# First block's attention taken by token tile, with keys and values of two heads laid side by side among zeros

## The chip, the cores and the metric

The kernel runs on one core of a Trainium2 chip. The metric is device time in microseconds of one launch, the median of three runs. A core has TensorE (PE in the rows; PEld is its weight load), VectorE (DVE), ScalarE (ACT) and GpSimd (POOL), which run side by side and wait for one another by semaphores, and SyncE (SP), whose queue issues nearly all transfers here.

## The reference

Chunked attention feeds a feed-forward layer with a rational activation, and that feeds a soft mixture of experts. All values are float32, except that the weights `w_in` and `w_out` arrive as float64.

```python
# attention: q, k, v of 4 x 8 heads x 768 x 64; chunks of 32 queries
k_full = concat([mem_k, k[chunk_start - 16 : chunk_end + 8]])   # 8 + up to 56 keys
a = softmax(scale * q_c @ k_full.T);  out = a @ v_full
# 3072 tokens x 512
h = x @ w_in                                                    # 2048 columns
g = (a0 + a1 h + a2 h^2 + a3 h^3) / (1 + |b0||h| + |b1|h^2 + 1e-6)
x = g @ w_out
# soft mixture of 8 experts: softmaxes of x @ phi over tokens and over slots
logits = x @ phi;  slots = softmax(logits, 0).T @ x
y = per expert relu(slots @ w1) @ w2;  out = softmax(logits, 1) @ y
```

## The kernel before

The 3072 tokens are taken in six blocks of 512. Each block has eight steps; a step makes 256 columns of `h` (the tile `h`, two times 128 rows by 512 tokens), runs the rational activation over them, and feeds the result to transposes and to the logits. Attention runs ahead: while block b goes through its steps, the attention of block b + 1 is fed in between in small slices (`at` in the order lists `ord0` and `ord`). A unit of attention is a pair, 256 tokens of 8 heads, thus two token tiles of 128.

The parts that the change and the prediction touch:

- **First attention.** Block 0 has no block ahead of it, so its two pairs (A and B in the list `pre`) run before the first step, with the engines' order written out by hand. `attention` (L151) multiplies 32 queries by 64 keys for one head at a time: 64 rows of contraction, 64 columns (L168). Two heads share the 128 partitions, one in each half, so per pair 64 such products give the scores. Each product in float32 runs as two passes. DVE takes the maximum and subtracts it (L186, L189), ACT takes the exponent (L190), PE turns the result (L208), ACT copies it out (L212), DVE forms sums and their reciprocals (L197 to L199), PE multiplies by the values (L228), DVE normalises (L238), PE turns (L246), and ACT copies into `xt` (L250), the block's x.
- **busy** (L285, `f` in `pre`): products with the identity that only keep TensorE going.
- **First h tile.** After the attention `h_part` (L380) makes the first `h` in one go, 16 passes of 512 columns.
- **Narrowing.** Each step of block 0 needs one float64 piece of `w_in` (letters i for its load, s and t for the first two conversions) and one of `w_out` turned (o, n). A conversion (`f64_narrow`, L303 to L307) is a scaling on ACT, a clamp on DVE, a second ACT pass and a combination on DVE, over a staging buffer `g` of which there are four. A piece is 1 MB in two transfers of 512 KB.
- **wp_sum** (L479, z): phi times the turned piece of `w_out`, two short groups of products with an ACT copy between them.
- **A step**: `a1` is three ACT passes over `h` (L607, L608, L610) and one on DVE, `d1` and `t` are DVE's polynomial (L619, L620, L632, L633) and POOL's product (L585), `a2` two more ACT passes (L624, L625). `h` of the next step is made during the step.

Before the first step the order is by hand; from there a scheduler sets the order by priorities and by pins (`issue_after`: not before a named instruction). Each engine runs its instructions strictly in that order, and the transfers are issued in order on SP.

Of the kernel before, what the change touches and what calls it, by code (L numbers as in the profile page):

```python
# [10 lines left out]
F32 = mybir.dt.float32  # L11
# [8 lines left out]
def float_of_bits(u):  # L20
# [3 lines left out]
KN = {  # L24
    'loads': "q0 q1 v0 i0 v1 c0 i1 o0 q2 v2 o1".split(),
    'pre': "f10 A A f5 B B A A A A B B A A B B A A A A s B B B B A A f2 A B B A s A B B A f2 B s B B B c f4 t t n n".split(),
    'pre2': "i2 o2 i3".split(),
    'ord0': "at a1 z0 s2 h0 d1 at t o3 i4 n1 at a2 y h1 p0 at p1 at at".split(),
    'ord': "at a1 h0 d1 at t a2 y x2 h1 p0 p1 x1 at x3 at at r".split(),
    'ordl': "a1 h0 d1 t a2 x2 h1 p0 p1 x1 x3 r".split(),  # L30
# [16 lines left out]
def tile_chunk_attention__rational__soft_moe(  # L47
# [64 lines left out]
    def bank(shape):  # L112
        return ps_m("m", shape)
# [15 lines left out]

    def load_qk(pair, tq=None, tk=None):  # L130
        if tq is None:
            tq, tk = p_q("q", [P, HP, 2 * P]), p_k("k", [P, HP, 8, WIN])
        SP.dma_start(out=tq, in_=qw[pair])
        for o in (slice(0, HP // 2), slice(HP // 2, HP)):
            SP.dma_start(out=tk[:, o], in_=kw[pair, :, o])
        ahead["q", pair] = tq, tk

    def load_v(pair, tv=None):
        if tv is None:
            t = p_v("v", [P, 2, 4, HP, D])  # L140
            tv = [t[:, n] for n in range(2)]
        for n in range(2):
            SP.dma_start(out=tv[n], in_=vwin[pair, :, n])
        ahead["v", pair] = tv
# [6 lines left out]
    def attention(pair, tile4=None, after=None):  # L151
        tile4 = tile4 or (lambda shape: p_a4("a4", shape))
        after = pair + 1 if after is None else after
        t_first = 2 * pair
        b = (t_first * P) // BLK
        qt, kt = ahead.pop(("q", pair))
        if pair < 2:
            both = ps_h("h", [P, 2, 2, HP, WIN])
            sc = [both[:, par] for par in range(2)]
        else:  # L160
            sc = [bank([P, 2, HP, WIN]) for _ in range(2)]
        for n in range(2):
            for hp in range(HP):
                for c in range(4):
                    for par in range(2):
                        r = slice(D * par, D * par + D)
                        o = P * n + CH * c
                        PE.matmul(  # L168
                            sc[par][CH * c:CH * c + CH, n, hp, :],
                            lhsT=qt[r, hp, o:o + CH],  # L170
                            rhs=kt[r, hp, 4 * n + c, :],
                            start=True, stop=True)
            yield
        if after < NPAIR:
            load_qk(after)
        pr = tile4([P, 2, HP, 2, WIN])
        rsum = []
        for par in range(2):
# [12 lines left out]
            yield  # L191
        pt = tile4([P, 2, HP, P])

# [20 lines left out]

        for part in (turns, sums) if pair < 2 else (sums, turns):
            yield from part()
        vt = ahead.pop(("v", pair))
        if pair < 2:
            both = ps_h("h", [P, 2, 2, HP, D])
            pv = [both[:, par] for par in range(2)]  # L220
        else:
            pv = [bank([P, 2, HP, D]) for _ in range(2)]
        for n in range(2):
# [11 lines left out]
            yield  # L235
        x_tok = tile4([P, 2, HP, 2, D])
        for par in range(2):
# [241 lines left out]
    def wp_sum(i):  # L479
# [11 lines left out]
    xtra = [p_xt("xt", [P, 2048]) for _ in range(2)]  # L491
    early = {"q": xtra[0][:, 0:1024].rearrange("p (h t) -> p h t", h=HP),
             "k": xtra[1].rearrange("p (h c j) -> p h c j", h=HP, c=8),
             }

    def load(what):
        kind, n = what[0], int(what[1])
        if kind == "q":
            if n == 1:
                load_qk(1, early["q"], early["k"])  # L500
            else:
                load_qk(n)
        elif kind == "v":
            load_v(n, [p_S("S", [P, 4, HP, D]) for _ in range(2)] if n == 1 else None)
        elif kind == "c":
            load_constants()
        elif kind == "i":
            load_w_in(n)
        elif kind == "o":
            load_w_turned(n)  # L510

    def convert(what):
        kind, n = what[0], int(what[1])
        if n < NSTEP:
            for _ in {"s": narrow_w_in, "n": narrow_w_turned, "z": wp_sum, "i": load_w_in, "o": load_w_turned}[kind](n) or ():
                pass

    new_xt(0)
    for what in KN["loads"]:
        load(what)  # L520
    gens = {"A": attention(0, after=NPAIR), "B": attention(1, lambda shape: p_T("T", shape), after=NPAIR),
            "s": narrow_w_in(0), "n": narrow_w_turned(0), "t": narrow_w_in(1), "c": constants()}
    for what in KN["pre"]:
# [8 lines left out]
    total = NBLK * NSTEP  # L532
    hs, gt_tile = {}, {}

    hs[0] = ps_h("h", [P, 2, BLK])
    h_part(0, hs[0], 0)
    h_part(0, hs[0], 1)
    for what in KN["pre2"]:
# [51 lines left out]
    def run_step(kk, what):  # L590
# [3 lines left out]
        if what == "at":  # L594
            slice_()
        elif what in ("h0", "h1"):
# [7 lines left out]
        elif what == "a1" and live:  # L604
# [3 lines left out]
            ACT.activation(y, hh, AF.Square, scale=rb1)  # L608
            DVE.scalar_tensor_tensor(s, y, QC, s, ALU.add, ALU.add)  # L609
            ACT.activation(t, hh, AF.Identity, bias=a2, scale=a3)  # L610
            act[kk] = s, t, y
# [262 lines left out]

_INS = ['qw', 'kw', 'vw', 'moe_w_in', 'moe_w_out', 'moe_a', 'moe_b', 'w_turned', 'moe2_phi', 'moe2_w1', 'moe2_w2']
_OUTS = [((3072, 512), 'float32')]


def _lay_out(inputs):
# [19 lines left out]
    qw = q.reshape(B, HP, 2, NP, 256, D).transpose(0, 3, 2, 5, 1, 4).reshape(B * NP, 128, HP, 256)  # L899
    kw = windows(k, mem_k).reshape(B, HP, 2, NP, 8, 64, D).transpose(0, 3, 2, 6, 1, 4, 5)  # L900
    kw = kw.reshape(B * NP, 128, HP, 8, 64)
    vw = windows(v, mem_v).reshape(B, HP, 2, NP, 2, 4, 64, D).transpose(0, 3, 2, 6, 4, 5, 1, 7)
# [5 lines left out]
    phi = np.asarray(inputs["moe2_phi"]).reshape(4, 128, 32).transpose(1, 0, 2).reshape(128, 128)  # L908
    return {**inputs, "moe2_phi": phi, "moe2_w2": w2, "qw": qw, "kw": kw, "vw": vw, "moe_w_in": w_in, "moe_w_out": w_out, "w_turned": w_turned}

# [24 lines left out]
```

## Time and profile before

| | us |
|---|---|
| median of three runs (576.18 to 576.56) | 576.53 |
| profiled execution, its own time | 577.91 |
| span of that execution, first to last instruction | 575.8 |
| PE busy / DVE / ACT / POOL | 540.6 / 456.3 / 427.9 / 122.2 |
| first activation of step 0 (block 0) starts | 38.68 |
| first activation of step 8 (block 1) starts | 133.26 |

The profile gives a page of totals, and the trace behind it answers by time: busy time of each engine in chosen stretches, instructions in order of time, and the chain of waits (the work that ended last, followed back). "Busy" of PE includes modelled ends of its pipelined products. A row of the timeline gives start, duration, engine, line, operation, written tile <- read tiles, shape, count, and in brackets how long the engine sat idle before it and what ended that.

### The profile page before, as it was taken

The page shows a single profiled execution, that of the slowest core. Times are in us where ns is not written, and L with a number is a line of the kernel's source. Part 1 is how long each engine was busy: PE and PEld are TensorE (multiplying, and loading weights), DVE is VectorE, ACT ScalarE, POOL GpSimd, SP SyncE. Part 2 cuts the span into 40 slices and gives each one's busy share as a digit, 9 for nine tenths or more (in the row PEclk, how much of TensorE's full clock was granted, in tenths as well). Part 3 has the DMA queues.
Part 4 walks back from the last instruction along what each step waited for, and adds up shares of the span by engine and source line. Part 5 has one row for each costly group of instructions (what it writes and reads, how often), then busy time and mean ns, then how long its engine had stood idle before and what let it go on. Part 6 is the DMA issues. An engine that isn't in the chain of part 4 may idle for free.

```text
span 575.8 us, 13647 instructions
## 1 busy us (share of the span) xinstructions
PE 540.6 (94%) x5874; PEld 362.1 (63%) x5874; DVE 456.3 (79%) x572; ACT 427.9 (74%) x551; POOL 122.2 (21%) x66
## 2 busy tenths in 40 slices
PE   6799897999999999999999999999999999999991
PEld 6644443557767767677766777776768767643351
DVE  3759988989898999979899799898898978831042
ACT  1489896897978999779787888896888978721132
POOL 0001111213221322313231313132223322300000
PEclk8799898999999999999999999999999999999996
DMA  8997854301125315341432335304349374799948
GB/s 319 361 382 256 279 189 162 137 12 56 56 76 183 129 56 183 115 170 36 161 111 74 114 107 184 110 12 174 110 145 372 106 252 150 268 392 410 409 173 357
DMA packets 28139, 105.80 MB, mean 184 GB/s; under 512 B 3376, under 2 KB 3504, under 8 KB 27056
## 3 DMA queue, kind: packets, MB, share of 16 engines
q1 hardware_dynamic: 26928, 100.74, 48.1%
q0 software_dynamic: 1152, 4.19, 1.8%
q8 instruction: 46, 0.75, 0.5%
q14 instruction: 13, 0.11, 0.0%
HBM read 94.44 MB, written 10.49 MB: 182 GB/s over the span
## 4 chain that ended last, share of the span: by engine, by line
PE 56%; DVE 15%; ACT 14%; DMA 8%; issue 4%; POOL 1%; ACTq 0%; SPq 0%; DVEq 0%; POOLq 0%
PE h L380 28%; DMA g<-in_w_turned_dram 5%; PE m L405 4%; PE m L458 4%; ACT S L607 3%; PE lg L398 3%; ACT S L608 3%; ACT g L406 3%; DVE T L619 3%; PE h L796 2%; PE m L228 2%; DVE T L620 2%; PE lg L833 2%; DMA g<-in_moe_w_in_dram 2%; DVE T L632 2%
## 5 line engine op out<-in xcount | busy, mean ns | idle before, releaser
L380 PE MATMUL h<-xt,win 128*128 128x512 f32 x1012 | 268.5, 414 | 0.7 <-DVE T L620 0.6
L380 PEld LDWEIGHTS h<-xt,win 128*128 128x128 f32 x1012 | 184.1, 188 | 50.9 <-issue 12.3
L585 POOL TENSOR_TENSOR S<-S,S 128x1024 f32<-128x1024 f32 x46 | 112.2, 2440 | 335.1 <-DVE S L609 282.1
L607 ACT ACTIVATE S<-h,ctab 128x1024 f32<-128x1024 f32 x47 | 52.5, 1117 | 38.3 <-PE h L380 37.5
L609 DVE SCALAR_TENSOR_TENSOR S<-S,S 128x1024 f32<-128x1024 f32 x47 | 57.3, 1220 | 24.3 <-ACT S L608 23.7
L619 DVE TENSOR_TENSOR T<-T,h 128x1024 f32<-128x1024 f32 x47 | 57.1, 1215 | 7.6 <-ACT T L610 7.6
L405 PEld LDWEIGHTS m<-ident,T 128*128 128x128 f32 x384 | 43.4, 141 | 29.4 <-issue 14.0
L620 DVE SCALAR_TENSOR_TENSOR T<-T,ctab,h 128x1024 f32<-128x1024 f32 x47 | 59.9, 1274 | 0.7
L632 DVE SCALAR_TENSOR_TENSOR T<-T,ctab,S 128x1024 f32<-128x1024 f32 x46 | 58.6, 1274 | 0.0
L633 DVE SCALAR_TENSOR_TENSOR T<-S,T 128x1024 f32<-128x1024 f32 x46 | 56.1, 1220 | 2.4 <-DVE T L632 0.5
L406 ACT ACTIVATE g<-m 128x512 f32<-128x512 f32 x96 | 53.2, 601 | 6.3 <-PE m L405 6.0
L610 ACT ACTIVATE T<-h,ctab 128x1024 f32<-128x1024 f32 x47 | 57.5, 1223 | 0.0
L625 ACT ACTIVATE S<-S,ctab 128x1024 f32<-128x1024 f32 x47 | 54.5, 1159 | 0.9
L624 ACT ACTIVATE S<-S 128x1024 f32<-128x1024 f32 x47 | 50.5, 1074 | 6.1 <-DVE S L609 6.1
L405 PE MATMUL m<-ident,T 128*128 128x128 f32 x384 | 53.0, 278 | 1.2 <-DVE a L189 1.2
L608 ACT ACTIVATE S<-h,ctab 128x1024 f32<-128x1024 f32 x47 | 52.7, 1121 | 0.9 <-DVE T L632 0.9
L380 PE MATMUL h<-xt,x 128*128 128x512 f32 x64 | 31.4, 621 | 3.6 <-DVE x L307 3.6
L398 PE MATMUL lg<-T,wp 128*32 128x512 f32 x192 | 33.1, 605 | 1.3 <-DVE T L633 0.7
L190 ACT ACTIVATE a<-a 128x512 f32<-128x512 f32 x22 | 13.4, 639 | 16.6 <-DVE a L189 16.6
L458 PE MATMUL m<-g,s 128*32 128x512 f32 x192 | 21.8, 595 | 0.4 <-ACT s L450 0.4
L303 ACT ACTIVATE g<-g 128x1024 uint32<-128x1024 uint32 x16 | 18.7, 1166 | 4.3 <-DMA g<-in_w_turned_dram 4.3
L380 PEld LDWEIGHTS h<-xt,x 128*128 128x128 f32 x64 | 11.2, 191 | 16.3 <-issue 15.1
(218 smaller groups left out, 673.5 us busy)
## 6 DMA issues: line engine op xcount, KB each, us to landing
win<-in_moe_w_dram SPq DMA_DIRECT2D x31, 512.0 KB, 7.3
k<-in_kw_dram SPq DMA_DIRECT2D x22, 512.0 KB, 6.3
v<-in_vw_dram SPq DMA_DIRECT2D x22, 512.0 KB, 5.2
g<-in_moe_w_in_dram SPq DMA_DIRECT2D x16, 512.0 KB, 7.3
g<-in_w_turned_dram SPq DMA_DIRECT2D x16, 512.0 KB, 6.5
x<-in_moe_w_out_dram SPq DMA_DIRECT2D x8, 1024.0 KB, 4.8
out_dram<-win SPq DMA_DIRECT2D x12, 512.0 KB, 5.0
q<-in_qw_dram SPq DMA_DIRECT2D x11, 512.0 KB, 3.8
```

Source lines behind the costliest of these rows:

```text
L380: PE.matmul(tile_[f2] if step == total - 1 else tile_[:, f2, :], lhsT=ww[:, c, f2 * P:f2 * P + P], rhs=xx[:, c, :], start=(n == 0), stop=( ...
L405: st["turn"] = PE.transpose(pb[:, m, f2 * P:f2 * P + P], t_[:, f2, tt * P:tt * P + P], ident)
L406: ACT.activation(gts[b, qd][:, 2 * part:2 * part + 2, 2 * P * o:2 * P * o + 2 * P], pb, AF.Copy)
L585: POOL.tensor_tensor(out, q, w, ALU.mult)
L607: ACT.activation(s, hh, AF.Abs, scale=b0)
L608: ACT.activation(y, hh, AF.Square, scale=rb1)
L609: DVE.scalar_tensor_tensor(s, y, QC, s, ALU.add, ALU.add)
L610: ACT.activation(t, hh, AF.Identity, bias=a2, scale=a3)
L619: DVE.tensor_tensor(t, t, hh, ALU.mult)
L620: behind[kk] = DVE.scalar_tensor_tensor(t, t, a1, hh, ALU.add, ALU.mult).ins
L632: DVE.scalar_tensor_tensor(t, t, a0, w, ALU.add, ALU.mult)
L633: st["t"] = DVE.scalar_tensor_tensor(t, e, 2.0, t, ALU.subtract, ALU.mult, reverse0=True).ins
```

## The change

- **By token tile.** Block 0's attention is done by a new function `attention_first`, once for each of the four token tiles (A, B, C, D in `pre`). Keys and values of a tile are laid into a buffer of twice the width: one head in the upper 64 partitions and the left half, the other in the lower 64 and the right half, zeros elsewhere. One product of 128 rows then serves both heads: 16 products of 128 columns for a tile's scores and 16 for its output, where it took 32 of 64 columns each.
- **Zeros and loads.** `clear` writes the zeros, two half-height memsets for each of eight buffers, one buffer on DVE and seven on POOL. Each key or value tile is loaded by two transfers of 64 partitions (256 KB each).
- **First h tile in halves** (`h_first`, H and J in `pre`): H makes the first half of the tokens once tiles 0 and 1 are done, J the second half, 16 passes of 256 columns each.
- **What is loaded and converted before step 0.** The order of loads is new; `w_in` goes ahead of `w_out`. Before, conversions i0, i1 and the first of `w_out` (n) were whole before step 0, and two more had begun. Now only i0 and i1 are converted before it, and `w_out`'s pieces run one step later, with wp_sum in the next step (Z).
- **Constants** come in one transfer with phi. `stack` is built by fewer instructions. `busy` has products of 256 columns.
- **Pins**: conversions stay behind the first activations of the step, the first slice behind J. From block 2 on each engine's order is unchanged.

```diff
 KN = {
-    'loads': "q0 q1 v0 i0 v1 c0 i1 o0 q2 v2 o1".split(),
...
+    'loads': "Q0 K0 K1 V0 Q1 K2 V1 K3 i0 V2 V3 c0 i1 q2 i2 v2 o0 i3".split(),
...
+    def clear(engine, t):
+        for par in range(2):
+            engine.memset(t[apart[par], 1 - par], 0.0)
...
+            for par in range(2):
+                SP.dma_start(out=t[apart[par], par], in_=src[apart[par]])
...
+    def attention_first(n):
+        o = P * (n % 2)
+        sc = ps_h("h", [P, HP, 2, WIN])
+        for hp in range(HP):
+            for c in range(4):
+                PE.matmul(sc[CH * c:CH * c + CH, hp], lhsT=q_first[n // 2][:, hp, o + CH * c:o + CH * c + CH],
+                          rhs=k_first[n][:, :, hp, c, :], start=True, stop=True)
+        yield
...
+        for hp in range(HP):
+            for c in range(4):
+                PE.matmul(pv[CH * c:CH * c + CH, hp], lhsT=pt[:, hp, CH * c:CH * c + CH],
+                          rhs=v_first[n][:, :, c, hp, :], start=True, stop=True)
+        yield
...
+    def h_first(half):
+        if 0 not in hs:
+            hs[0] = ps_h("h", [P, 2, BLK])
+        o = slice(P // 2 * half, P // 2 * half + P // 2)
...
+            for c in range(NC):
+                pins["PE"] = PE.matmul(to[:, :, o], lhsT=w_f[0][:, c, f2 * P:f2 * P + P], rhs=x[:, c, :, o],
+                                       start=(c == 0), stop=(c == NC - 1)).ins
...
+    clear(DVE, k_first[0])
+    for t in (k_first[1], v_first[0], k_first[2], v_first[1], k_first[3], v_first[2], v_first[3]):
+        clear(POOL, t)
...
-        SP.dma_start(out=ctab[:, 0:4], in_=ca.unsqueeze(0).to_broadcast([P, 4]))
-        SP.dma_start(out=ctab[:, 4:6], in_=cb.unsqueeze(0).to_broadcast([P, 2]))
-        SP.dma_start(out=u_acc[:, 0:NC * NSLOT], in_=phi)
+        SP.dma_start(out=u_all[:, BLK - NC * NSLOT:BLK + 6], in_=cst)
...
-    h_part(0, hs[0], 0)
-    h_part(0, hs[0], 1)
...
+        elif what == "Z":
+            if 0 < kk <= NSTEP:
+                convert("z" + str(kk - 1))
```

TensorE's order at the end of the first attention, before: `a_3`, `T_543` are the normalised outputs of pairs A and B, `h_584` the first h tile.

```order
L208 MATMUL m_445<-ident_106,T_340 128x128 x4
L288 MATMUL lg_463<-ident_106 128x128 x2
L246 MATMUL m_466<-ident_106,a_3_460 128x128 x4
L228 MATMUL h_471<-S_158,T_439 32x64 x32
L228 MATMUL h_471<-S_159,T_439 32x64 x32
L246 MATMUL m_538<-ident_106,a_3_460 128x128 x4
L288 MATMUL lg_547<-ident_106 128x128 x2
L246 MATMUL m_550<-ident_106,T_543 128x128 x4
L246 MATMUL m_556<-ident_106,T_543 128x128 x4
L288 MATMUL lg_569<-ident_106 128x128 x4
L380 MATMUL h_584<-xt_143,win_435 128x512 x8
```

The same place now: `x_126` holds the keys of tile 3, `x_125` and `g_127` are the values of tiles 2 and 3, `a_3` and `a_4` their outputs, `h_423` the first h tile.

```order
L265 MATMUL h_347<-x_126,S_161 32x128 x16
L281 MATMUL m_364<-ident_106,T_336 128x128 x4
L357 MATMUL lg_375<-ident_106 128x256
L281 MATMUL m_382<-ident_106,T_379 128x128 x4
L293 MATMUL h_397<-x_125,S_369 32x128 x16
L301 MATMUL m_417<-ident_106,a_3_414 128x128 x4
L318 MATMUL h_423<-xt_119,win_393 128x4x64 x8
L293 MATMUL h_432<-g_127,S_387 32x128 x16
L301 MATMUL m_451<-ident_106,a_4_449 128x128 x4
L318 MATMUL h_423<-xt_119,win_393 128x4x64 x8
```

The first half of the h tile has moved ahead of tile 3's products with the values and its last transposes; these wait behind it.

ScalarE's order up to the first activation of step 0, before: `g_165` is the second `w_in` piece, `g_168` and `g_179` the first two of `w_out`.

```order
L275 ACTIVATE ctab_108<-ctab_108 128x2
L278 ACTIVATE ctab_108<-ctab_108 128x1
L279 ACTIVATE ctab_108<-ctab_108 128x1
L303 ACTIVATE g_165<-g_165 128x1024
L305 ACTIVATE g_165<-g_165 128x1024
L303 ACTIVATE g_168<-g_168 128x1024
L305 ACTIVATE g_168<-g_168 128x1024
L303 ACTIVATE g_179<-g_179 128x1024
L607 ACTIVATE S_638<-h_584,ctab_108 128x1024
```

And now: `g_169` is the first piece of `w_in`, `g_177` the second, `S_387` tile 3's turned weights, `u_109` holds the constants.

```order
L277 ACTIVATE T_379<-T_379 128x512
L284 ACTIVATE S_387<-m_382 128x512
L372 ACTIVATE g_169<-g_169 128x1024
L374 ACTIVATE g_169<-g_169 128x1024
L305 ACTIVATE xt_119<-m_417 128x16x32
L305 ACTIVATE xt_119<-m_451 128x16x32
L344 ACTIVATE u_109<-u_109 128x2
L347 ACTIVATE u_109<-u_109 128x1
L348 ACTIVATE u_109<-u_109 128x1
L372 ACTIVATE g_177<-g_177 128x1024
L374 ACTIVATE g_177<-g_177 128x1024
L660 ACTIVATE S_514<-h_423,u_109 128x1024
```

The conversion of the first `w_in` piece now stands behind tile 3's copy, and the three passes over `w_out`'s pieces have moved behind the first activation.

## Rows read from the trace of the kernel before

**Rows 1.** Busy time in stretches: block 0 from step 0 on, block 1.

```profile
core 0: us, PE busy (x) PEld busy (x) DVE busy (x) ACT busy (x) POOL busy (x), PEclk, DMA share, GB/s
...
38.68:133.26 94.58, 86.13 (x772) 44.47 (x768) 85.41 (x95) 84.61 (x107) 18.39 (x7) 0.96 0.50 174
133.26:209.00 75.74, 75.33 (x886) 54.28 (x879) 70.60 (x86) 65.70 (x84) 19.29 (x8) 1.00 0.29 99
```

**Rows 2.** Chain of waits, the start: start, us, what.

```profile
1.17 5.70 DMA k<-in_kw_dram
...
6.88 11.52 DMA g<-in_moe_w_in_dram
```

**Rows 3.** Timeline of TensorE: start, us, engine, line, operation, tiles, shapes, count.

```profile
23.44 1.06 PE L288 MATMUL lg<-ident 128*128 128x128 f32 x4
...
27.26 0.66 PE L246 MATMUL m<-ident,a 128*128 128x128 f32 x4
...
29.64 1.06 PE L288 MATMUL lg<-ident 128*128 128x128 f32 x8
...
30.54 7.13 PE L380 MATMUL h<-xt,win 128*128 128x512 f32 x16
...
37.60 0.86 PE L168 MATMUL m<-k,q 64*32 64x64 f32 x64
...
38.96 1.98 PE L380 MATMUL h<-xt,win 128*128 128x512 f32 x4
...
162.78 3.64 PE L458 MATMUL m<-g,s 128*32 128x512 f32 x32
```

**Rows 4.** Timeline of VectorE and ScalarE: first attention, narrowing, first activations.

```profile
9.74 0.69 DVE L186 TENSOR_REDUCE mx<-h 128x8 f32<-128x512 f32 x1
...
11.19 0.63 ACT L190 ACTIVATE a<-a 128x512 f32<-128x512 f32 x1 [9.17 <-DVE a L189]
...
18.90 0.63 DVE L197 TENSOR_REDUCE sm<-a 128x8 f32<-128x512 f32 x1
...
19.77 0.20 DVE L199 RECIPROCAL sm<-sm 128x8 f32<-128x8 f32 x1
...
22.50 1.24 DVE L238 TENSOR_TENSOR a<-h,sm 128x512 f32<-128x512 f32 x2
...
22.83 0.60 ACT L212 ACTIVATE T<-m 128x512 f32<-128x512 f32 x1 [1.08 <-PE m L208]
...
31.14 1.15 ACT L303 ACTIVATE g<-g 128x1024 uint32<-128x1024 uint32 x1
...
31.80 0.70 DVE L304 TENSOR_SCALAR g<-g 128x1024 f32<-128x1024 f32 x1
...
32.54 1.13 ACT L305 ACTIVATE g<-g 128x1024 f32<-128x1024 f32 x1 [0.24 <-DVE g L304]
...
33.70 1.23 DVE L307 SCALAR_TENSOR_TENSOR win<-g 128x1024 uint32<-128x1024 uint32 x1 [1.20 <-ACT g L305]
...
38.68 1.10 ACT L607 ACTIVATE S<-h,ctab 128x1024 f32<-128x1024 f32 x1
...
133.26 1.12 ACT L607 ACTIVATE S<-h,ctab 128x1024 f32<-128x1024 f32 x1
```

**Rows 5.** Busy time in stretches of 2 us of the first attention, columns as in rows 1.

```profile
18.00:20.00 2.00, 0.61 (x56) 0.45 (x41) 1.86 (x7) 1.77 (x3) 0.00 (x0) 0.82 0.56 184
...
22.00:24.00 2.00, 2.00 (x11) 2.00 (x10) 1.93 (x6) 0.92 (x2) 0.00 (x0) 0.50 1.01 383
...
26.00:28.00 2.00, 1.95 (x103) 1.69 (x97) 0.64 (x2) 0.05 (x1) 0.00 (x0) 0.97 1.04 422
```

**Rows 6.** Groups by line and shape on GpSimd: count, busy us, mean ns.

```profile
L760 POOL MEMSET wp<- 128x512 f32 x1 | 0.5, 528 | 6.4 <-PE lg L398 6.4
```

**Rows 7.** Timeline in block 0: a wait for a transfer and the one it caused.

```profile
90.88 1.18 ACT L303 ACTIVATE g<-g 128x1024 uint32<-128x1024 uint32 x1 [3.42 <-DMA g<-in_w_turned_dram]
...
97.66 1.06 PE L380 MATMUL h<-xt,x 128*128 128x512 f32 x1 [3.56 <-DVE x L307]
```

More of the change, by code (lines that the diff above doesn't have):

```diff
@@ L149, in new_xt, with attention @@
         xt[b] = [p_xt("xt", [P, NC, BLK], F32R if b else F32) for _ in range(2 if b else 1)]
-    def attention(pair, tile4=None, after=None):
-        tile4 = tile4 or (lambda shape: p_a4("a4", shape))
-        after = pair + 1 if after is None else after
+    def attention(pair):
+        after = pair + 1
         t_first = 2 * pair
@@ L156, in attention @@
         qt, kt = ahead.pop(("q", pair))
[L157 to L161, printed above, removed]
+        sc = [bank([P, 2, HP, WIN]) for _ in range(2)]
         for n in range(2):
@@ L175, in attention @@
             load_qk(after)
[L176 removed]
+        pr = p_a4("a4", [P, 2, HP, 2, WIN])
         rsum = []
@@ L191, in attention @@
             yield
-        pt = tile4([P, 2, HP, P])
+        pt = p_a4("a4", [P, 2, HP, P])
         def sums():
@@ L213, in turns @@
             yield
-        for part in (turns, sums) if pair < 2 else (sums, turns):
-            yield from part()
+        yield from sums()
+        yield from turns()
         vt = ahead.pop(("v", pair))
[L218 to L222, printed above, removed]
+        pv = [bank([P, 2, HP, D]) for _ in range(2)]
         for n in range(2):
@@ L489, in wp_sum @@
         ACT.activation(wp[:, 2 * i:2 * i + 2, :], pb, AF.Copy)
[L491 to L494, printed above, removed]
     def load(what):
         kind, n = what[0], int(what[1])
[L498 to L510, printed above, removed]
+        if kind in "QKV":
+            load_first(kind, n)
+        else:
+            {"q": load_qk, "v": load_v, "c": lambda n: load_constants(), "i": load_w_in, "o": load_w_turned}[kind](n)
     def convert(what):
@@ L514, in convert @@
         if n < NSTEP:
-            for _ in {"s": narrow_w_in, "n": narrow_w_turned, "z": wp_sum, "i": load_w_in, "o": load_w_turned}[kind](n) or ():
-                pass
-    new_xt(0)
+            with tc.issue_after(pins[0]) if 0 in pins else nullcontext(), tc.issue_after(pins[1]) if 0 in pins else nullcontext():
+                for _ in {"s": narrow_w_in, "n": narrow_w_turned, "z": wp_sum, "i": load_w_in, "o": load_w_turned}[kind](n) or ():
+                    pass
     for what in KN["loads"]:
         load(what)
-    gens = {"A": attention(0, after=NPAIR), "B": attention(1, lambda shape: p_T("T", shape), after=NPAIR),
-            "s": narrow_w_in(0), "n": narrow_w_turned(0), "t": narrow_w_in(1), "c": constants()}
+    gens = {"ABCD"[n]: attention_first(n) for n in range(4)}
+    gens.update({"H": h_first(0), "J": h_first(1), "s": narrow_w_in(0), "t": narrow_w_in(1), "c": constants()})
     for what in KN["pre"]:
@@ L594, in run_step @@
         if what == "at":
-            slice_()
+            with tc.issue_after(pins["PE"]) if kk == 0 else nullcontext():
+                slice_()
         elif what in ("h0", "h1"):
@@ L608, in run_step @@
             ACT.activation(y, hh, AF.Square, scale=rb1)
-            DVE.scalar_tensor_tensor(s, y, QC, s, ALU.add, ALU.add)
-            ACT.activation(t, hh, AF.Identity, bias=a2, scale=a3)
+            pins[0] = DVE.scalar_tensor_tensor(s, y, QC, s, ALU.add, ALU.add).ins
+            pins[1] = ACT.activation(t, hh, AF.Identity, bias=a2, scale=a3).ins
             act[kk] = s, t, y
@@ L908, in _lay_out @@
     phi = np.asarray(inputs["moe2_phi"]).reshape(4, 128, 32).transpose(1, 0, 2).reshape(128, 128)
-    return {**inputs, "moe2_phi": phi, "moe2_w2": w2, "qw": qw, "kw": kw, "vw": vw, "moe_w_in": w_in, "moe_w_out": w_out, "w_turned": w_turned}
+    cst = np.concatenate([phi] + [np.tile(np.asarray(inputs[n]), (128, 1)) for n in ("moe_a", "moe_b")], axis=1)
+    return {**inputs, "cst": cst, "moe2_w2": w2, "qw": qw, "kw": kw, "vw": vw, "moe_w_in": w_in, "moe_w_out": w_out, "w_turned": w_turned}
 def kernel(**inputs):
```

118 lines of the change are left out of this document (81 added, 37 removed).

## The prediction

> **What bounds the kernel now.** I read the stretches first. In block 1 PE is busy 75.33 of 75.74 us [rows 1], and from block 2 on no engine's order changes: what counts is when PE comes to its dense work, and how much it stands still on the way. In block 0, from its first activation at 38.68 to that of block 1 at 133.26 [rows 4], no engine is full: PE 86.13, DVE 85.41 and ACT 84.61 of 94.58 us [rows 1]. The three hand work to one another, so about 8 to 10 us stand idle on each. One piece of that has a name: ACT waits 3.42 us for a piece of `w_out`, and behind it PE 3.56 us for weights that DVE combines late [rows 7]. Ahead of block 0 the chain of waits shows transfers alone: one issued at 1.17 and landed at 6.87, the next issued at 6.88 and landed at 18.40 [rows 2]. By order of the loads 1024 KB had landed by then and 5120 KB by the second, so 512 KB take 11.53 / 8 = 1.44 us. On the engines the first h tile runs from 30.54 to 37.67, and that of step 1 starts at 38.96 [rows 3].
>
> **The products themselves.** A pair's half of scores, 64 passes of 64 columns, takes 0.86 us [rows 3]. The new form is 32 passes of 128 columns by 128 rows and 32 weight columns. The nearest row is L458, with the same 128 rows and 32 weight columns: 32 passes of 512 columns in 3.64 us [rows 3], 4500 columns per us, which gives 4096 / 4500 = 0.91 us. So half as many instructions stream as many columns in as much time; between 0.43 (time goes by instructions) and 1.72 (the columns of two heads no longer overlap) I take 0.9. [...]
>
> **The first attention, step by step.** Durations [rows 3, 4]: products 0.9; maximum and subtraction 1.45 (9.74 to 11.19); exponent 0.63; four transposes 0.65; copy 0.60; sums 1.07 (18.90 to 19.97); normalising 0.62; narrowing 1.15 + 1.13 on ACT and 0.70 + 1.23 on DVE. Loads land at 1.44 us per 512 KB from 6.9 on: keys 1 at 8.3, keys 2 with queries at 12.7, keys 3 at 15.5, the first `w_in` piece at 18.4, values 3 at 21.3. A memset of 512 columns takes 0.53 on POOL [rows 6]; 14 of 1024 columns, at twice that, end at 16, before the values they belong to, so the zeros cost nothing. (On a slower POOL, at 1.5 each, they would end at 22, still before tile 3's values are used.)
> Tile 0: scores 6.9 to 7.8, subtracted by 9.35, exponent 10.0, turned 10.65. ACT works in order, so its copy waits for tile 1's exponent (11.45) and ends at 12.05; values 12.95, normalised 13.6. PE then does tile 2's scores (13.85), turns tile 1 (14.5) and tile 0's output (15.15); tile 1's values 16.05, normalised 16.7, turned 17.35. Tile 3's scores end at 18.25, subtracted 19.7, exponent 20.35, turned 21.0, copied 21.6. Only then does ACT come to the first `w_in` piece, landed 3 us before: 22.75, second pass 23.9, DVE's combination 25.1. H follows. A pass of 512 columns takes 7.13 / 16 = 0.45 us [rows 3], so 256 take at least 0.22; with the weight loads closer together I take 0.25, H 4.0 us, to 29.1. Behind H: tile 3's values 30.0, normalised 30.65, turned 31.3, copied 31.9, J to 35.9. In that time ACT does the constants (0.9) and both passes of the second `w_in` piece, to 35.1, DVE's combination to 36.3. The first activation starts at 35.9, not 38.68. PE does the first scores of the next pair (0.86) and starts step 1's h at 36.8, not 38.96: **2.2 us earlier**. Bounds: H and J at 0.22 a pass give 3.1; the other end is the clock, below.
>
> **What block 0 has to take over.** Three ACT passes (2 x 1.15 + 1.13 = 3.4 us) and on DVE three clamps and one combination (2.1 + 1.2), less one combination that falls into block 1, thus 2.1 us, move behind the first activation. They cost between nothing (10.0 us on ACT and 9.2 on DVE are idle there [rows 1]) and 3.4; as both engines are about 90% full, I take half, 1.7. The last wp_sum moves into block 1 and is paid there by a PE that is full: no gain. Against this, `w_in` pieces are now asked for ahead of `w_out`, and the conversion of `w_out` has a step more. SP's queue holds the piece of step 3 and then that of step 4 before the second of `w_out`. The wait of 3.4 to 3.6 us [rows 7] should go; between 0 and 3.6 I take 3.0, since the next to come late, DVE with its 9.2 us of slack, is near. Block 0 gives **1.3 us**. The one transfer of constants in place of three, the shorter `stack` and the pins lie before 6.9 us or beside waits for transfers: nothing.
>
> **The sum.** 2.2 + 1.3 = 3.5 us. The profiled execution took 577.91 us (span 575.8 and 2.1 around it), so it would take 574.4; it stands 1.4 above the median of the runs, 576.53, which becomes 573.0.
>
> **Rivals.**
> *H at half clock: slower.* H starts after PE has had little to do, and tile 3's last products stand behind it in PE's order. [...] At half clock H's passes take 0.43, not 0.25: 2.9 us more for H, as much for J. If 19 of the 32 passes run so, the 3.5 us are gone; with all, the median is 573.0 + 5.8 = 578.8. Against it: there is product work in every 2 us up to H. [...]
> *Twice the product time: slower.* If the 128-row products take 1.72, seven of the eight lie on the chain above, 7 x 0.8 = 5.7 us: median 578.7. L458 speaks against it.
> *Given back: no change.* If ACT is what bounds block 0, the whole 3.4 us lands, and of the wait for `w_out` only 1.2 comes free, as it turns into one for ACT: 2.2 - 3.4 + 1.2 = 0, 576.5. For it: of ACT's 10.0 us of idle time in block 0 [rows 1] a third is that one wait [rows 7], so the rest of the time it is fuller than DVE or PE. Against it: ACT's moved passes spread over eight steps.
> *More: block 0 flows.* If early weights take away half to all of PE's 8.45 us of idle time [rows 1], it gives 4 to 8 us in place of 1.3: 566.5 to 570.3. DVE's and ACT's fill speaks against it.
>
> **How the numbers follow.** Forecast 0.53 (569.8 to 575.3), more 0.16, given back 0.13 (within 0.2%, about what a measurement of this kernel can tell from no change: 575.4 to 577.7), half clock 0.14, doubled products 0.04. Faster 0.69, same 0.13, slower 0.18. The range 567.0 to 578.8 reaches through the clock rival's full price and most of "more" and leaves out about 2 in 10.
>
> **What would show it.** Step 0's first activation near 36, step 1's h near 37. A granted clock near 1.0 in the stretch of H (25 to 29) and rows of 0.25 for its passes against the clock rival; 32 passes of L265 in 0.9 us against the doubled products. Block 0 from first activation to first activation about 93 us, no wait of ACT for `w_out` above 1 us. The forecast is wrong if DVE or ACT idles in block 0 less than now and yet the block takes 95 us or more, or if the first activation lies past 38.

## The result and the profile after

The changed kernel takes 584.72 us (median; 584.23 to 589.53), the kernel before 576.54 on the same chip: ratio 1.0147, 95% interval 1.0114 to 1.0179. It is 1.5% slower, above the whole range of the prediction. The profiled execution took 585.19 us, 7.3 more than the one before.

The starts of the first activations divide the loss; "first" is that of step 0.

| us | before | after | difference |
|---|---|---|---|
| first | 38.68 | 42.52 | +3.84 |
| block 0 (step 0 to step 8) | 94.58 | 94.59 | 0.0 |
| steps 8 and 9 | 19.78 | 21.06 | +1.3 |
| steps 10 to 15 | 58.29 | 60.21 | +1.9 |
| blocks 2 to 5 and the end, to the last instruction | | | +0.5 |

Stretches of the kernel after; columns are stretch, length, busy time (and count) of PE, PEld, DVE, ACT, POOL, then granted clock, DMA share and GB/s. First three stretches of the prologue, one of H, then block 0, steps 8 and 9, steps 10 to 15:

```profile
6.00:8.00 2.00, 0.96 (x32) 0.84 (x32) 0.00 (x0) 0.00 (x0) 1.91 (x3) 1.00 1.04 229
12.00:14.00 2.00, 0.90 (x32) 0.84 (x32) 1.90 (x5) 1.00 (x2) 1.91 (x3) 1.00 1.03 231
16.00:18.00 2.00, 1.70 (x35) 1.30 (x28) 1.38 (x2) 0.91 (x2) 0.00 (x0) 1.00 1.01 231
...
30.00:32.00 2.00, 1.89 (x7) 1.34 (x6) 0.77 (x1) 0.60 (x1) 0.00 (x0) 0.50 1.01 395
...
42.52:137.11 94.59, 87.10 (x844) 44.86 (x843) 89.67 (x99) 87.27 (x108) 16.66 (x7) 1.00 0.53 182
137.11:158.17 21.06, 18.97 (x212) 13.64 (x211) 18.71 (x22) 17.49 (x23) 5.66 (x2) 0.92 0.22 77
158.17:218.38 60.21, 59.39 (x697) 41.90 (x703) 53.45 (x67) 51.09 (x66) 14.44 (x6) 1.00 0.28 97
```

The first and the last two of them in the kernel before:

```profile
6.00:8.00 2.00, 0.46 (x32) 0.33 (x32) 0.00 (x0) 0.00 (x0) 0.00 (x0) 1.00 1.03 414
...
133.26:153.04 19.78, 19.78 (x222) 14.09 (x215) 18.92 (x23) 16.86 (x22) 4.84 (x2) 1.00 0.25 82
153.04:211.33 58.29, 57.88 (x697) 41.87 (x702) 53.90 (x66) 50.98 (x66) 14.45 (x6) 1.00 0.29 100
```

Three things are to be seen. In the prologue the DMA engines are as busy as before (share above 1.0) and move 229 to 231 GB/s, not 414 (or the 422 of [rows 5]). In steps 8 and 9 PE stands still for 2.1 us and its clock is 0.92. In steps 10 to 15 PE does the same work with the same count of products (697), but is busy 1.5 us longer.

The chain of waits at the start (start, us, what) answers to [rows 2]; the transfer of tile 2's values lands at 15.16 + 11.66 = 26.82:

```profile
6.10 9.04 DMA xt<-in_kw_dram
15.16 11.66 DMA x<-in_vw_dram
```

PE's timeline behind that (as [rows 3]): values of tile 2, H, values of tile 3, J, the next pair's scores, step 1's h.

```profile
26.96 1.94 PE L293 MATMUL h<-x,S 128*32 128x128 f32 x32 [2.27 <-DMA x<-in_vw_dram]
29.70 1.11 PE L301 MATMUL m<-ident,a 128*128 128x128 f32 x4 [0.81 <-DVE a L297]
30.92 4.67 PE L318 MATMUL h<-xt,win 128*128 128x256 f32 x16
35.52 1.08 PE L293 MATMUL h<-g,S 128*32 128x128 f32 x32
...
38.76 3.72 PE L318 MATMUL h<-xt,win 128*128 128x256 f32 x16 [0.69 <-ACT xt L305]
42.41 0.86 PE L158 MATMUL m<-k,q 64*32 64x64 f32 x64
43.30 3.24 PE L449 MATMUL h<-xt,win 128*128 128x512 f32 x7
```

H stood behind tile 2's values, for which PE waited 2.27 us. It then ran its first 2.0 us (30.92 to 32.90) at a granted clock of 0.50 and took 4.67 us, where J takes 3.72 at 1.00.

### The profile page after: what moved, and what is told of

The parts are those of the page before. It is cut to its first block, busy times and chain, and to the rows that moved or that the text cites. A ratio compares the mean times of both kernels' runs of the same rounds, so it can differ in the third digit from the quotient of the medians.

```text
span 583.3 us, 13135 instructions
## 1 busy us (share of the span) xinstructions
PE 541.5 (93%) x5604; PEld 360.3 (62%) x5604; DVE 457.7 (78%) x561; ACT 428.1 (73%) x551; POOL 134.5 (23%) x80
## 4 chain that ended last, share of the span: by engine, by line
PE 54%; DVE 18%; ACT 15%; issue 5%; DMA 4%; POOL 2%; SPq 1%; ACTq 0%; DVEq 0%; POOLq 0%
PE h L449 25%; PE m L527 4%; PE m L474 4%; ACT S L660 3%; ACT S L661 3%; PE lg L467 3%; ACT g L475 3%; DVE S L662 3%; DVE T L673 3%; DVE T L672 3%; PE h L852 2%; PE m L214 2%; PE lg L889 2%; DVE T L685 2%; DMA x<-in_vw_dram 2%
## 5 line engine op out<-in xcount | busy, mean ns | idle before, releaser
L449 PE MATMUL h<-xt,win 128*128 128x512 f32 x996 | 259.2, 409 | 1.7 <-issue 0.8
L449 PEld LDWEIGHTS h<-xt,win 128*128 128x128 f32 x996 | 181.0, 188 | 49.3 <-issue 11.1
L660 ACT ACTIVATE S<-h,u 128x1024 f32<-128x1024 f32 x47 | 52.5, 1118 | 40.9 <-PE h L449 38.0
L673 DVE SCALAR_TENSOR_TENSOR T<-T,u,h 128x1024 f32<-128x1024 f32 x47 | 59.8, 1272 | 0.7
L685 DVE SCALAR_TENSOR_TENSOR T<-T,u,S 128x1024 f32<-128x1024 f32 x46 | 58.6, 1274 | 0.0
L663 ACT ACTIVATE T<-h,u 128x1024 f32<-128x1024 f32 x47 | 57.5, 1224 | 0.0
L678 ACT ACTIVATE S<-S,u 128x1024 f32<-128x1024 f32 x47 | 54.3, 1156 | 1.0
L661 ACT ACTIVATE S<-h,u 128x1024 f32<-128x1024 f32 x47 | 52.7, 1122 | 0.6 <-DVE T L685 0.6
L467 PE MATMUL lg<-T,wp 128*32 128x512 f32 x192 | 38.3, 604 | 1.8 <-DVE T L686 1.3
L374 ACT ACTIVATE g<-g 128x1024 f32<-128x1024 f32 x16 | 18.6, 1160 | 2.3 <-DVE g L373 2.3
```

What stands on the lines that cost most here:

```text
L449: PE.matmul(tile_[f2] if step == total - 1 else tile_[:, f2, :], lhsT=ww[:, c, f2 * P:f2 * P + P], rhs=xx[:, c, :], start=(n == 0), stop=( ...
L660: ACT.activation(s, hh, AF.Abs, scale=b0)
L663: pins[1] = ACT.activation(t, hh, AF.Identity, bias=a2, scale=a3).ins
L673: behind[kk] = DVE.scalar_tensor_tensor(t, t, a1, hh, ALU.add, ALU.mult).ins
```

## The experiments

All were timed in alternation with the kernel before, whose median beside them was 576.5 to 577.9 us; so runs are compared by the ratio to it. Stretches are of one profiled execution each.

| | median | ratio (95%) | first | block 0 | steps 8-9 | steps 10-15 |
|---|---|---|---|---|---|---|
| before | 576.54 | | 38.68 | 94.58 | 19.78 | 58.29 |
| after | 584.72 | 1.0147 (1.0114 to 1.0179) | 42.52 | 94.59 | 21.06 | 60.21 |
| e1 two queues | 585.28 | 1.0139 (1.0107 to 1.0172) | 44.40 | 92.27 | 20.70 | 60.21 |
| e2 before, key halves | 580.44 | 1.0051 (1.0032 to 1.0069) | 41.92 | 93.50 | 19.78 | 58.35 |
| e3 values ahead of H | 581.83 | 1.0075 (1.0048 to 1.0101) | 39.64 | 92.03 | 20.73 | 60.23 |
| e4 old conversions | 589.96 | 1.0221 (1.0162 to 1.0279) | 41.72 | 98.84 | 19.13 | 60.23 |
| e5 even and odd partitions | 583.09 | 1.0083 (1.0061 to 1.0105) | 40.83 | 94.20 | 21.37 | 60.67 |
| e6 quartets whole | 589.22 | 1.0199 (1.0157 to 1.0241) | 43.88 | 95.15 | 22.62 | 58.22 |
| e7 before, quartets whole | 579.44 | 1.0032 (1.0016 to 1.0048) | 39.39 | 94.51 | 19.71 | 58.56 |
| e8 e3 + e5 + e6 | 581.00 | 1.0052 (1.0032 to 1.0072) | 36.31 | 93.97 | 22.18 | 58.19 |
| e9 wp_sum's copy first | 586.25 | 1.0142 (1.0121 to 1.0163) | 44.16 | 94.16 | 20.01 | 60.49 |
| e10 e8 + e9, blocks 0, 1 | 578.52 | 1.0015 (1.0001 to 1.0029) | 37.93 | 93.57 | 16.53 | 62.75 |
| e11 fill ahead of H | 592.34 | 1.0223 (1.0186 to 1.0260) | 46.45 | 98.65 | 16.14 | 65.30 |
| e12 e3 + e5 | 578.52 | 1.0013 (0.9994 to 1.0032) | 36.23 | 92.04 | 20.72 | 60.24 |
| e13 e12 + block 1's quartets | 575.58 | 0.9965 (0.9946 to 0.9983) | 36.06 | 92.04 | 20.75 | 58.09 |
| e14 e13 + e9 | 575.09 | 0.9952 (0.9933 to 0.9971) | 37.50 | 92.06 | 19.99 | 58.32 |

After, e6 and e9 have the same order on every engine up to step 0, and their first activations lie at 42.52, 43.88 and 44.16: what is under 1.7 us in that column is not told from chance in one execution.

### The transfers: e2, e1, e5

e2 cuts the first keys by partitions in the kernel before (`D` is 64, `P` 128).

```diff
-        for o in (slice(0, HP // 2), slice(HP // 2, HP)):
-            SP.dma_start(out=tk[:, o], in_=kw[pair, :, o])
+        for o in [(slice(0, D),), (slice(D, P),)] if pair < 2 else [(slice(0, P), slice(0, HP // 2)), (slice(0, P), slice(HP // 2, HP))]:
+            SP.dma_start(out=tk[o], in_=kw[(pair,) + o])
```

> The kernel before, with one edit: the four 512 KB transfers of keys (pairs 0 and 1) are cut by partitions, 64 x 2048, and not by heads, 128 x 1024: the same bytes, number, size and queue. Ports theory: 2 MB at 230 in place of 414 GB/s take 4.1 us more, the first w_in piece lands at 22.4 and not at 18.4, the first activation comes at 42.7 and not at 38.7, and the kernel takes 580 to 581 us. Size theory: the pieces are as large as before, so nothing changes, 576.5.

Windows of e2, of the keys and after them:

```profile
6.00:8.00 2.00, 0.27 (x2) 0.14 (x2) 0.00 (x0) 0.00 (x0) 0.00 (x0) 1.00 1.04 223
...
16.00:18.00 2.00, 1.00 (x62) 0.76 (x57) 0.00 (x0) 0.00 (x0) 0.00 (x0) 0.50 1.02 404
```

Same bytes, number, size and queue: 223 GB/s while the halves move, 404 afterwards, first activation 3.2 us and the kernel 0.51% later. By the landings in the traces a half of 512 KB took 2.3 to 2.5 us here; in the kernel before 512 KB to 128 partitions took 1.3. The size theory falls.

e1 asks for the upper halves from ACT's queue.

```diff
-                SP.dma_start(out=t[apart[par], par], in_=src[apart[par]])
+                (ACT if par else SP).dma_start(out=t[apart[par], par], in_=src[apart[par]])
...
-    start.enter_context(tc.manual_schedule(engines={e.engine for e in (PE, ACT, DVE, POOL)}))
+    start.enter_context(tc.manual_schedule(engines={e.engine for e in (PE, ACT, DVE, POOL, SP)}))
```

> The changed kernel; of each first tile of keys and values the upper 64 partitions are asked for from ACT's queue and the lower 64 from SP's, so that both are under way at once; SP's order is otherwise kept. Ports theory (a transfer to 64 partitions moves at about 230 GB/s, one to 128 at about 414, both read in the traces): the windows from 4 to 20 us go back to about 400 GB/s, the values of tile 2 land near 20 and not at 26.8, step 0's first activation comes at 37 to 38 and not at 42.5, and the kernel takes 579 to 581 us, since block 1 keeps its loss. Size theory (the 256 KB pieces are slow because they are small and at most eight are outstanding): nothing changes, 230 GB/s, 42.5, 584.7. Order theory (H waits for its weights and tile 3's values stand behind it): the loads get faster, but the first activation stays above 41 and the time above 583.

```profile
6.00:8.00 2.00, 0.00 (x1) 0.03 (x1) 0.00 (x0) 0.00 (x0) 1.91 (x3) 0.98 1.01 244
...
12.00:14.00 2.00, 0.85 (x11) 0.30 (x2) 1.38 (x2) 0.00 (x0) 1.91 (x3) 1.00 1.06 287
```

In these windows the rate is 244 and 287 GB/s (the second also holds queries for 128 partitions). The twelfth half lands at 19.74, in the kernel after at 19.51, and the time is that of the kernel after: two halves that are under way together still don't add up to a whole. My form of the ports theory was wrong in that. At most 287 GB/s were measured, against 414 to 422 for transfers to 128 partitions in the kernel before. The eight of the size theory are in the trace: in the kernel after at most eight of SP's transfers lie between issue and landing at a time.

e5 puts one head on the even and the other on the odd partitions. The tiles are cleared whole ahead of the transfers, q is laid out on the host to match, and DVE writes the subtracted scores interleaved.

```diff
-                SP.dma_start(out=t[apart[par], par], in_=src[apart[par]])
+                SP.dma_start(out=t[par:P:2, par], in_=src[apart[par]])
...
```

> The changed kernel with the two heads of a pair on even and odd partitions and not on the lower and upper 64: each transfer still brings 256 KB to 64 partitions, as many and as large, but spread over all 128. The tiles are cleared whole ahead of their transfers, keys of tiles 0 and 1 by DVE, and DVE writes the subtracted scores interleaved. The order of PE's work is the same as in the changed kernel from block 0 on. Ports theory: windows from 6 to 18 us at about 400 GB/s, the values of tile 2 in by 18 to 20, step 0's first activation at 37 to 39 (42.5 before this edit), and the kernel at 579.5 to 581, since the loss of blocks 0 and 1 stays. Rival (a transfer to 64 partitions is slow whichever they are): 230 to 250 GB/s as before, first activation 42 to 44, 584 to 587.

```profile
6.00:8.00 2.00, 0.94 (x32) 0.84 (x32) 0.00 (x0) 0.00 (x0) 2.00 (x2) 1.00 0.72 229
...
12.00:14.00 2.00, 2.00 (x8) 1.43 (x7) 1.90 (x6) 0.92 (x2) 0.00 (x0) 0.50 0.94 350
14.00:16.00 2.00, 2.00 (x50) 1.58 (x52) 1.11 (x5) 0.21 (x1) 0.00 (x0) 0.70 0.95 356
16.00:18.00 2.00, 1.72 (x36) 1.30 (x25) 1.78 (x3) 0.68 (x2) 0.00 (x0) 1.00 0.98 342
...
20.00:22.00 2.00, 2.00 (x41) 1.63 (x42) 1.18 (x4) 0.60 (x1) 0.00 (x0) 1.00 1.04 407
```

Still 64 partitions and 256 KB a transfer, now 342 to 356 GB/s at shares of 0.94 to 0.98, and 407 from 20 to 22, when values of tiles 2 and 3 land, a transfer every 0.64 us (every 1.1 in the kernel after). From 6 to 8 the engines are busy for 0.72 alone: the transfers are issued behind the zeros, which now fill whole tiles. So it is which partitions, not how many: 64 neighbouring ones were filled at 223 to 231 GB/s, every second one at 342 to 407. Why that is so, no run here shows. The kernel won less than expected (583.09, not 581; first activation at 40.83, not 37 to 39). PE waited 1.62 us for H's weights, and H took 5.38 us behind that wait, most of it at a low clock (0.71 granted from 28 to 30, 0.50 from 30 to 32, 0.93 from 32 to 34):

```profile
28.53 5.38 PE L318 MATMUL h<-xt,win 128*128 128x256 f32 x16 [1.62 <-DVE win L377]
```

### The order of H: e3, e11

```diff
-D C C f1 D D D s C C s C C H H D D D D J J c t t
+D C C f1 D D D s C C s C C D D H H D D J J c t t
```

> The changed kernel with tile 3's values and their normalising ahead of the first half of h in the hand-written order. Order theory: tile 3's products, 1.1 us, run while H waits for its weights, the chain behind H loses products, normalising and turning, and the first activation comes 2 us earlier, at 40.5; 582.7 us. Ports theory: those values land late as well (about 29 us), so at most 1 us is saved: 41.5 to 42.5, 583.7 to 584.7.

PE's timeline in e3:

```profile
30.02 1.08 PE L293 MATMUL h<-g,S 128*32 128x128 f32 x32
31.03 3.72 PE L318 MATMUL h<-xt,win 128*128 128x256 f32 x16
34.59 0.60 PE L301 MATMUL m<-ident,a 128*128 128x128 f32 x4
35.88 3.72 PE L318 MATMUL h<-xt,win 128*128 128x256 f32 x16 [0.69 <-ACT xt L305]
```

The values of tile 3 landed in time; tile 3's products fill the wait, H follows at once and takes 3.72 us, as J did at a granted clock of 1.00, and J comes 2.9 us earlier. Block 0 is 2.5 us shorter as well, in e3 and in e12 to e14 alike, where the scheduler's order of block 0 differs too. Other runs separate this from the earlier end of tile 3: e1 leaves tile 3's values behind H, has another order in block 0 and takes 92.27; e5 has the order of the kernel after there, starts 1.7 us earlier and takes 94.20; e8 and e10 have tile 3's values ahead of H and yet other orders, and take 94.0 and 93.6. The length goes with the scheduler's order.

e11 fills the wait with eight idle products (16 passes) instead (`C C f8 H H`).

> The changed kernel with eight idle passes of 256 columns on PE ahead of the first half of h, in the time in which PE waits for its weights. Clock theory (H runs at half clock because PE had little to do, and this is the loss): H takes 3.7 us and not 4.67, as J does; the first activation comes 1 to 3 us earlier, at 39.5 to 41.5. Ports theory: H gets to the full clock, but the loads still set its start and that of J; the first activation moves by 1 us at most, 41.5 to 42.5, and the kernel stays at 583.5 to 585.

```profile
30.97 5.10 PE L357 MATMUL lg<-ident 128*128 128x256 f32 x16
35.90 3.62 PE L318 MATMUL h<-xt,win 128*128 128x256 f32 x16
```

H is fast, as the clock theory says, but the idle products themselves took 5.10 us and pushed H back by 5; first activation and kernel lie above what either theory expected. The low clock of H costs 1 us; buying it off with idle work cost more.

### Block 1: e4, e9, e6, e7

In steps 8 and 9 of the kernel after, PE (first) waits for ACT (second), which waits for POOL: the last `wp_sum` (L552, L554, L557).

```profile
141.79 0.63 PE L552 MATMUL m<-win,u 128*32 128x256 f32 x8
142.25 1.02 PE L467 MATMUL lg<-T,wp 128*32 128x512 f32 x2
145.35 0.92 PE L557 MATMUL m<-stack,s 128*128 128x32 f32 x4 [2.09 <-ACT s L554]
146.20 2.05 PE L158 MATMUL m<-k,q 64*32 64x64 f32 x128
```

```profile
143.91 1.11 ACT L660 ACTIVATE S<-h,u 128x1024 f32<-128x1024 f32 x1 [1.60 <-POOL S L637]
144.93 0.38 ACT L554 ACTIVATE s<-m 128x256 f32<-128x256 f32 x1
```

e4 takes the conversions of block 0 back to the old order (lists `loads`, `pre`, `pre2`, `ord0`, `ord`).

> The changed kernel with the order of block 0's conversions of before: the first w_out piece is narrowed ahead of block 0 again, the others a step earlier, wp_sum in the step of its own piece, and the last wp_sum again inside block 0. Spill theory (block 1's 3.2 us come from the last narrowing and wp_sum that fall into it): block 1 goes back from 81.3 to about 78 us, the first activation stays near 42.5 to 44, and the kernel takes 581 to 583 us. Rival (block 1's stall is the scheduler's order of steps 8 and 9 or the attention's, not that piece): block 1 stays near 81 and the kernel at 584 to 587.

Steps 8 and 9 take 19.13, so the spill is one cause; but steps 10 to 15 stay at 60.23, and block 0 takes 98.84, 4.2 more than after. The kernel, 589.96, lies above both ranges. Taking the deferral back, which I had priced as a cost of 1.7 us, was no gain; where e4 loses in block 0 was not followed.

e9 only orders ACT: the copy ahead of step 9's activation.

```diff
-        ACT.activation(part, pb, AF.Copy)
+        st["ws"] = ACT.activation(part, pb, AF.Copy).ins
...
-            ACT.activation(s, hh, AF.Abs, scale=b0)
+            with tc.issue_after(st["ws"]) if kk == NSTEP + 1 else nullcontext():
+                ACT.activation(s, hh, AF.Abs, scale=b0)
```

> The changed kernel with one rule more: on ACT, the first activation of step 9 (L660) is issued behind the copy of the last wp_sum (L554). In the changed kernel it stands ahead of it and waits 1.60 us for POOL, the copy behind it, and PE, whose second half of wp_sum needs the copy, stands still for 2.09 us and then works at a lower clock (0.88 in that step); steps 8 and 9 take 21.06 us, 19.78 in the kernel before. Spill theory: that wait of PE falls under 1 us, steps 8 and 9 take 19.5 to 20.3, and the kernel 583 to 583.8. Rival (whatever holds PE there is replaced by the next: POOL, DVE's narrowing): steps 8 and 9 stay at 21, 584.7.

PE in e9 at the same place:

```profile
143.46 1.02 PE L467 MATMUL lg<-T,wp 128*32 128x512 f32 x2
144.41 0.63 PE L557 MATMUL m<-stack,s 128*128 128x32 f32 x4
144.97 1.48 PE L158 MATMUL m<-k,q 64*32 64x64 f32 x128
```

No wait, a granted clock of 1.00 in the two steps (the 128 passes of scores take 1.48 and not 2.05 us), and 20.01 for them: the spill theory holds for 1.0 us. The kernel's time doesn't show it (ratio 1.0142, 1.0147 after); the stretch does. In the profiled execution the first activation came 1.6 us later than after.

The rest is in the slot logits, four products of 32 weight columns that can run beside one another. Each shows as two rows. First after, then before:

```profile
195.85 1.04 PE L467 MATMUL lg<-T,wp 128*32 128x512 f32 x2
196.83 0.66 PE L198 MATMUL m<-ident,a 128*128 128x128 f32 x4
197.42 1.06 PE L467 MATMUL lg<-T,wp 128*32 128x512 f32 x6
```

```profile
190.84 1.06 PE L398 MATMUL lg<-T,wp 128*32 128x512 f32 x8
```

One product alone takes 1.04 us, three take 1.06, and all four 1.06. The scheduler's new order breaks the quartets more often. Groups by line, after (L467) and before (L398); count, busy us, mean ns, idle before:

```profile
L467 PE MATMUL lg<-T,wp 128*32 128x512 f32 x192 | 38.3, 604 | 1.8 <-DVE T L686 1.3 <-DVE T L766 0.6
```

```profile
L398 PE MATMUL lg<-T,wp 128*32 128x512 f32 x192 | 33.1, 605 | 1.3 <-DVE T L633 0.7 <-DVE T L710 0.6
```

5.2 us more for the same 192 passes: five pieces more, all ahead of block 2, two of them in steps 10 to 15 (six where there were four). e6 and e7 write the quartets in another order, in the kernel after and before.

```diff
-                for j in range(4):
+                for j in (2, 3, 0, 1):
```

> The changed kernel with one token changed: the four products of a quartet of slot logits (L467) are written in the order 2, 3, 0, 1, so that the one that is written first is one whose operand comes last, and the scheduler has no reason to start the quartet early and break it. In the traces a broken quartet takes 1.05 us for each piece, and a whole one 1.06; the changed kernel has 5 pieces more than the kernel before, all ahead of block 2. Quartets theory (block 1's 3.2 us are 3 such pieces on a full PE, and 2 more fill block 0): L467's sum over the kernel goes from 38.3 to about 33 us, block 1 goes from 81.3 to about 78, the first activation stays at 42 to 43, and the kernel takes 580 to 581.5. Spill theory (the last wp_sum in block 1 makes the loss): block 1 stays at 80 to 81, the kernel at 583 to 585.

> The kernel before with the same token changed (its L398). Its quartets are broken 2 and 2 once in block 0, and once a block in blocks 1 to 5 with 1 and 3. Quartets theory: two pieces fewer ahead of block 3, 2 us of PE time, one of them in full blocks: 574.5 to 575.5. Spill theory: no change, 576.5.

```profile
L467 PE MATMUL lg<-T,wp 128*32 128x512 f32 x192 | 29.7, 604 | 6.5 <-DVE T L686 5.9 <-DVE T L766 0.6
```

In e6 the quartets' sum fell by 8.6 us (5 were expected) and steps 10 to 15 by 2.0; but ahead of the quartets PE now waits 5.9 us for DVE (2.4 of it in blocks 2 to 5, 1.7 in the last steps; 1.3 in the whole kernel after), and in steps 8 and 9 the wait for `wp_sum` grew from 2.1 to 2.9 us, since pieces of a quartet had filled part of it. Both kernels got slower. Only in steps 10 to 15 of e6 was the token a gain.

### Together: e8, e10, e12 to e14

> The changed kernel with heads on even and odd partitions, tile 3's values ahead of H, and the quartets of logits in the order 2, 3, 0, 1. If both theories hold the gains add: first activation at 36 to 37.5, block 0 at 92 to 94, block 1 at 78: 574 to 576, under the kernel before. If only the ports theory holds: 578 to 580. If only the quartets theory holds: 578.5 to 580.

> The changed kernel with heads on even and odd partitions, tile 3's values ahead of H, the rule on the last wp_sum, and the quartets of logits in the order 2, 3, 0, 1 in blocks 0 and 1 alone (in later blocks that order made PE wait for DVE). First activation 36.3 to 37.5, steps 8 and 9 at 19.5 to 20.5 (22.2 with the quartets and without the rule), steps 10 to 15 at 58.2, the later blocks as in the kernel before: 574 to 576, under the kernel before by 0.2 to 0.6%. If the rule on wp_sum doesn't hold: 577 to 579.

e8's 581.00 lies above all three ranges. Its first activation at 36.31 is 6.2 us earlier than after, where e5 and e3 alone give 1.7 and 2.9: together the prologue's two edits win more than apart. Its 22.18 shows that the token hurts elsewhere. In e10 the stall left steps 8 and 9 (16.53) and came back behind them (62.75): 79.28 together, 2 under after, 1.2 above before, and the kernel's 578.52 misses 574 to 576.

> The changed kernel with only the two edits of the prologue: heads on even and odd partitions, and tile 3's values ahead of H. If the prologue's and the later losses are apart from one another: first activation 36.3 to 37.9, block 0 at 92 (as with tile 3's values ahead alone), steps 8 to 15 still at 81, so 575 to 577, the time of the kernel before, or 0.2% under it. If what the prologue gains is taken up by block 0 (94 to 95): 577.5 to 579.

> The same, with the quartets of logits of block 1 alone in the order 2, 3, 0, 1; all of PE's order up to step 8 and nearly all from block 2 on are as in the kernel without it. Quartets theory (broken quartets cost 1.9 us in steps 10 to 15): steps 10 to 15 take 58.2 in place of 60.2, nothing else moves: 1.5 to 2.5 us less than the kernel without it. Rival (with the quartets whole, PE waits for DVE as it did when all blocks had the order): less than 0.7 us less.

> The same with, besides, the rule on the last wp_sum (copy ahead of step 9's first activation on ACT). Steps 8 and 9 a further 1 us shorter (19.7 to 20.2) if the stall doesn't come back in step 10: 573 to 574.5. If the next wait takes its place, as it did when the rule and the quartets of blocks 0 and 1 were together: the same time as without the rule.

Steps 10 to 15 in e12 and in e13:

```profile
148.99:209.23 60.24, 60.24 (x696) 41.96 (x702) 54.05 (x68) 51.08 (x66) 14.44 (x6) 1.00 0.29 97
```

```profile
148.85:206.94 58.09, 56.97 (x725) 42.01 (x724) 54.75 (x68) 51.30 (x66) 14.46 (x6) 1.00 0.29 101
```

e12 undoes the prologue's loss: first activation 36.23, block 0 92.04, and the kernel is level with the one before. Its median lies in the range of the other case, though block 0 did not take the gain up: step 16 begins 2.1 us earlier than before, and part of that goes at the end, where the closing stores took 6.1 us each from issue to landing in place of 5.0. That was not followed. e13 changes one token for block 1: PE was full for 60.24 of 60.24 us and is busy 56.97 now, 2.2 us less in the stretch and 2.9 in the median. That settles the quartets for steps 10 to 15; the median moved by more than the range of 1.5 to 2.5. e14 with the rule on ACT is 0.48% faster than the kernel before (0.29 to 0.67%); over e13 it gains 0.8 us in steps 8 and 9 and nothing that the medians can tell apart, the second of its two cases.

## Why the prediction was wrong

**The step that failed** is the pace of the loads. I read 1.44 us per 512 KB from transfers to 128 partitions [rows 2] and used it for transfers to 64, which took 1.1 us per 256 KB. Tile 2's values should have landed near 19.8 and landed at 26.82; H was to start at 25.1 and started at 30.92; the first activation was to come at 35.9 and came at 42.52. The diff showed the 64 partitions, and the trace of before had no such transfer among the big ones: the price had to be bounded from both sides, and I took one end for it without saying so.

The pace is not the whole of it. e5 spreads the loads and keeps the forecast's order of H; H started at 28.53 and the first activation came at 40.83. Of the 5.8 us by which H was late, that gives back 2.4. Of the 3.4 left, some 1.2 are e5's own: its zeros fill whole tiles, and tile 1's keys, issued behind them, landed at 9.50, not 8.3. The other 2.2 lie in the steps of the attention, which took longer than forecast, and were not taken apart. That e12 comes to 36.23, near 35.9, is luck:

```profile
27.65 3.69 PE L318 MATMUL h<-xt,win 128*128 128x256 f32 x16 [0.67 <-DVE win L377]
```

There too H starts 2.5 us late, waiting for its weights, and the way behind it is shorter than forecast, as tile 3's values come ahead of H. By single executions the pace is worth 1.7 us (e5 against after) to 3.4 (e12 against e3), and the order of H 2.9 (e3 against after) to 4.6 (e12 against e5).

**Block 1** was priced at "no gain" for the `wp_sum` that moves there. It lost 3.2 us: about 1 by the wait of `wp_sum`'s second half behind ACT and POOL (e9, e4), 1.9 by broken quartets (e13, e6). The second I did not look for: I took the order from block 2 on as unchanged and did not read what the scheduler did in blocks 0 and 1.

**Block 0** was to give 1.3 us and gave none. The wait for `w_out` did go [rows 7] (0.6 us is left), but DVE and ACT are busy 4.3 and 2.7 us more than in [rows 1]. That looks like the rival "given back", but ACT's time is not the bound: e12, with ACT busy for 87.23 us as here, took 92.04. The runs with this order of block 0 (e5, e6, e9) take 94.2 to 95.2, those with another in e1, e3 and e12 to e14 92.0 to 92.3. The term failed by the order that the scheduler made of block 0, which the forecast did not look at; which instruction of it costs the time was not followed.

**Products** took 1.08 us at a granted clock of 1.00 and not 0.9, on seven of them 1.3 us; the rival of doubled products (1.72) fell. The shape of L458 was the right row, a fifth too cheap.

**The clock rival** was right in kind, and [rows 5] had shown the 0.50 it speaks of. Behind waits of 2.27 and 0.81 us H took 0.29 us a pass: its passes start 0.43 us apart at a granted clock of 0.50 and 0.22 apart at 1.00. The low clock cost 1 us of H (1.7 in e5) and nothing of J, not the 5.8 of the slower case.

By the terms: 6.5 us at step 1's h (2.2 earlier was forecast, 43.30 against 38.96 came), 0.8 from there to step 8 (1.3 less was forecast, 93.81 against 94.30 came), 3.2 in block 1 and 0.5 behind it make 11.0. Less 0.2 that the execution spent outside its span, that is the 10.8 between the forecast of 574.4 and the 585.19 measured.

## What to carry to other kernels

When a layout splits tiles over partitions, price its transfers by the partitions that each one reaches (64 neighbouring ones: 223 to 231 GB/s here), and keep each spread over all 128 even where it fills only half: every second partition moved as fast as all once the engines were full (407 GB/s at a share of 1.04 in e5, 414 at 1.03 before). When code ahead of a scheduled part changes, compare the order inside the groups of products that run side by side; a broken group paid its full time for every piece (1.04 us for one product of four, 1.06 for all four). A rearranged order is best judged in stretches between fixed points of the program, since gains and losses of 2 us in different stages hid one another here.

## What the hardware showed that I had not expected

- Halves of 64 neighbouring partitions moved at 223 to 231 GB/s with the DMA engines' share above 1.0; transfers as large to every second partition at 342 to 356 with a share of 0.94 to 0.98 and at 407 with 1.04; the share alone doesn't tell a slow transfer from a fast one.
- Asking for the two halves from two queues gave 244 to 287 GB/s, not twice the 223 to 231.
- One of four products with 32 weight columns took as long (1.04 us) as four together (1.06).
- A wait of 2 us of PE was followed by 128 passes of scores in 2.05 us, where without the wait they took 1.48 (granted clock of the two steps 0.92 and 1.00).
